# Inverse softmax sums carried as rows through DRAM, and two raw weight pieces fetched first, in a one-core attention and feed-forward kernel

## The chip, the cores and the metric

The kernel runs on one core of a Trainium2 chip. The metric is the device time of one execution in microseconds; the time of a kernel is the median of several runs. The engines are called as the profile calls them: PE (TensorE matmuls), PEld (its weight loads), DVE (VectorE), ACT (ScalarE), POOL (GpSimd) and SP (SyncE, which issues every DMA of this program, in order).

## The reference, cut to what matters

```python
# 8 batches x 8 heads, 576 positions, head size 64, all float32
scores = scale * q @ k.T
cum = np.cumsum(np.log(np.clip(f, 1e-4, 1)), axis=-1)
scores = where(causal, -1e9, scores + cum[..., :, None] - cum[..., None, :])
attn = np.exp(scores - scores.max(-1, keepdims=True))
attn = attn / (attn.sum(-1, keepdims=True) + 1e-9)
x = (attn @ v) -> (4608 tokens, 512)
h = x @ w_in            # 512 -> 2048
out = np.maximum(0.01 * h, h) @ w_out   # 2048 -> 512
```

The division by the row sums is what the change moves. Softmax itself is not normalised when the probabilities are made: the kernel multiplies the finished product `attn @ v` by the inverse sums.

## The kernel before, in words

**Exactness by halves.** A float32 operand is split into a rounded part (`_h`, `ph`, `gh`, `xh`) and a remainder (`_l`, `pl`, `gl`, `xs`), and a product takes two or three matmuls. The weights arrive as 64-bit words. `load_weight(n)` makes the two float32 halves of one piece (there are 16, each of 512 KB, alternately from `w_in` and `w_out`): two DMAs into a buffer `wraw`, one ACT operation (L150) and one ACT cast (L155), and six DVE operations of 1024 columns (L151, L152, L156, L158, L162, L163).

**Opening.** While the first data arrive PE runs dummy matmuls (`warm`, L105). Then come 12 pairs of *early heads* (three batches, the first 256 positions; `early_load`, `early_scores`, `early_values`), with the weight pieces made between them: one piece beside each of the first eight pairs, two beside each of the last four. `early_load` brings `qk` and `ve`; `early_scores` needs `qk` and the decay operand `both`.

**Main part.** 64 tasks follow, one a head; a step of the loop handles the scores of task t and the values of task t-1. For row blocks i = 0 to 4 the step runs `transposes(t-1, i)` and `scores(t, i)`, with pieces of feed-forward work between them (`fill`), then `values(t-1)` on PE, then `split(t+1)`, which makes the halves of the next head's operands and copies some of them by DMA into `fixed_s2a/b` and `fixed_m2a/b`. 24 tasks (of the batches whose first 256 positions were done early) start at block 2; their 12 pairs are called *narrow* here (320 columns), the other 20 pairs *wide* (576 columns). Two heads share an output tile `x` (64 partitions each).

**Inverse sums.** ACT's exponential (L366) leaves the row sums of both heads of a pair in `fixed["sum"]`, positions on the partitions. The products stand the other way round, positions along the columns. Before the change `inverse` takes the reciprocal on DVE (L440, L441, 128x10) and lets POOL repeat each number 64 times into a tile `rw` (L448); `normalise` then transposes `rw` on PE, one 128x128 transpose for each 128 positions, into PSUM tiles `rb` of the tag `tr` (L459), and DVE multiplies `x` by them (L460). The result goes by DMA to `xd` in DRAM (L464), from which the feed-forward part fetches groups of 256 tokens (`xs`, L475).

**Feed-forward.** `ffn` yields small quanta: `h` matmuls (L508, 128x256), an ACT activation, the halves `gh` (DVE, L518) and `gl` (POOL, L520), and `o` matmuls (L541, 128x512). A fixed rule (`fill`) sets how many quanta stand after each block.

**Order.** Within an engine instructions run in the order in which they stand in the program. That order is made by a scheduler with costs of its own, so a change in one place can move instructions elsewhere.

Of the kernel before, what the change touches and what calls it, by code (L numbers as in the profile page):

```python
# [29 lines left out]
RAWS = ("ph", "pl")  # L30
# [6 lines left out]
def forgetting_attention_ffn(ctx, tc, qT, kT, v4, vr, f, w_in, w_out, out):  # L37
# [6 lines left out]
    nc = tc.nc  # L44
    NHEAD, D, S = qT.shape
# [4 lines left out]
    NFULL = S // P  # L50
    REST = S - NFULL * P
    NCH = NFULL + 1
# [59 lines left out]
    ident = ident_r.bitcast(F32)  # L112
# [6 lines left out]
    )  # L119

    xd = dram.tile([DM, NTOK], F32, name="xd")
    dec_k, dec_q = (dram.tile([NHEAD, 2, S], F32, name=n) for n in ("dec_k", "dec_q"))

    fr = one.tile([2 * NHEAD, S], F32, tag="z4", name="fr")
# [6 lines left out]
    wpieces, loaded = [], []  # L131
    wi, wo = w_in.bitcast(I32), w_out.bitcast(I32)
    for p in range(NFC // 2):
        wpieces.append(((wi[p, 0], wi[p, 1]), win_h[p], win_l[p]))
        wpieces.append(((wo[2 * p], wo[2 * p + 1]), wout_h[p], wout_l[p]))

    def load_weight(n):


        loaded.append(n)  # L140
        srcs, wh, wl = wpieces[n]
        wh, wl = (w.rearrange("p c f -> p (c f)") for w in (wh, wl))
        raw = one.tile([P, 2, 4 * P, 2], I32, tag=RAWS[n % 2], name=f"wraw_{n}")
        for k, src in enumerate(srcs):
            nc.sync.dma_start(raw[:, k].rearrange("p w two -> p (w two)"), src)
        raw = raw.rearrange("p m w two -> p (m w) two")
        lo, hi = raw[:, :, 0], raw[:, :, 1]
        t = one.tile([P, 8 * P], I32, tag="vs", name=f"wt_{n}")
        tf = t.bitcast(F32)
        nc.scalar.activation(tf, hi.bitcast(F32), AF.Abs, scale=REBIAS)  # L150
        nc.vector.tensor_scalar(t, t, 3, None, op0=ALU.logical_shift_left)  # L151
        nc.vector.scalar_tensor_tensor(  # L152
            t, hi, -0x80000000, t, op0=ALU.bitwise_and, op1=ALU.bitwise_or
        )
        nc.scalar.copy(wh, tf)  # L155
        nc.vector.tensor_scalar(hi, t, -0x800000, None, op0=ALU.bitwise_and)  # L156
        rest = lo.bitcast(F32)
        nc.vector.scalar_tensor_tensor(  # L158
            rest, lo.bitcast(U32), 2.0**-52, hi.bitcast(F32), op0=ALU.mult, op1=ALU.mult
        )  # L160
        hi = hi.bitcast(F32)
        nc.vector.tensor_tensor(hi, tf, wh.bitcast(F32), op=ALU.subtract)  # L162
        nc.vector.tensor_tensor(wl, hi, rest, op=ALU.add)  # L163

    def weights(n):
        while len(loaded) < min(n, len(wpieces)):
            load_weight(len(loaded))
# [23 lines left out]
    for i in range(NCH):  # L191
        c = slice(i * P, width(i))
# [3 lines left out]
    for name, tag, x, to in (("fck", "s1", fc, dec_k), ("fcq", "m1", start, dec_q)):  # L196
        r = one.tile([P, S], F32R, tag=tag, name=name, bufs=2)
# [5 lines left out]
    pairs = {}  # L203
# [95 lines left out]
    fixed = {}  # L299
# [38 lines left out]
    def scores(t, i):  # L338

        s, c0, c1 = tasks[t]  # L340
        h = state[t]
        m, n = rows(i), width(i)
        if i < NFULL:
            z = h[f"z{i}"] = one.tile([P, n], F32, tag=f"z{i}", name=f"z{i}_{t}")
        else:
            z = h[f"z{i}"] = fixed["z4"]
        z = z[:m, :n]
        if i == c0:
            h["max"] = one.tile([P, NCH + 1], F32, tag="max", name=f"max_{t}", bufs=3)
        parts = [(0, n)] if n <= 512 else [(0, n // 2), (n // 2, n)]  # L350
        for x, (a, b) in enumerate(parts):
            ps = psum.tile([P, 512], F32, tag="sc", name=f"sc_{t}_{i}_{x}")
            cols = slice(i * P, i * P + m)
            for y, w in enumerate("12"):
                nc.tensor.matmul(  # L355
                    ps[:m, :b - a], h["s" + w][:, cols], h["m" + w][:, a:b],
                    start=y == 0, stop=y == 1,
                )
            at = TRI - P - i * P + a
            nc.vector.tensor_tensor_reduce(  # L360
                out=z[:, a:b], in0=ps[:m, :b - a], in1=tri[:m, at:at + b - a], scale=-SCALE,
                scalar=3.0e38 if x == 0 else h["max"][:m, i:i + 1],
                op0=ALU.add, op1=ALU.min, accum_out=h["max"][:m, i + x:i + x + 1],
            )
        last = i + len(parts) - 1
        nc.scalar.activation(  # L366
            z, z, AF.Exp, bias=h["max"][:m, last:last + 1], scale=-1.0,
            accum_out=fixed["sum" + "ab"[s // 2 % 2]][:m, i, s % 2:s % 2 + 1],
        )
# [65 lines left out]

    def inverse(t):

        s, c0, c1 = tasks[t]
        r = one.tile([P, NCH, 2], F32, tag="r", name=f"r_{t}")
        nc.vector.tensor_scalar(r, fixed["sum" + "ab"[s // 2 % 2]], 1.0e-9, None, op0=ALU.add)  # L440
        nc.vector.reciprocal(r, r)  # L441
        wide = pairs[s // 2, c0]["r"] = {}
        for lo, hi in spans(t):
            c = (hi - lo + P - 1) // P
            w = one.tile([P, c, 2, D], F32, tag=f"part{lo == 0:d}", name=f"rw_{t}_{lo}")
            a = r[:, lo // P:lo // P + c]
            a = bass.AP(tensor=a.tensor, offset=a.offset, ap=[*a.ap, [0, D]])
            nc.gpsimd.tensor_copy(w, a)  # L448
            wide[lo] = w.rearrange("p c o d -> p c (o d)")

    def normalise(t):

        s, c0, c1 = tasks[t]
        pair = pairs[s // 2, c0]
        x, r = pair["x"], pair["r"]
        for part, (lo, hi) in enumerate(spans(t)):
            ps = psum.tile([P, 512], F32, tag="tr", name=f"rb_{t}_{part}")
            for c in range(lo, hi, P):
                nc.tensor.transpose(ps[:, c - lo:c - lo + P], r[lo][:, (c - lo) // P], ident)  # L459
            nc.vector.tensor_tensor(x[:, lo:hi], x[:, lo:hi], ps[:, :hi - lo], op=ALU.mult)  # L460
        b, hp = s // HPB, (s % HPB) // 2
        a, n = c0 * P, width(c1 - 1)
        at = place[b, a]
        nc.sync.dma_start(xd[hp * P:(hp + 1) * P, at:at + n - a], x[:, a:n])  # L464

    def spans(t):
        a, n = tasks[t][1] * P, width(tasks[t][2] - 1)
        return [(a, n)] if n - a <= 512 else [(a + P, n), (a, a + P)]
# [137 lines left out]
    for t in range(nt + 1):  # L606
        heads[0] = t < nt
        if t + 1 < nt:
            load(t + 1)
        before = list(range(*tasks[t - 1][1:])) if t else []  # L610
        now = list(range(*tasks[t][1:])) if t < nt else []
        have = ready[0] // T * NQ - used[0]
        left = min((e + 2 - t for e in ends if e + 1 >= t), default=1)
        step = min(have / (left + SLACK), MAXQ) / 8
        fill(step)
        for i in range(5):
            if i in before:
                transposes(t - 1, i)
            if i in now:
                scores(t, i)  # L620
            fill(step)
        if t:
            for part in range(len(spans(t - 1))):
                if part == 0 and tasks[t - 1][0] % 2:
                    inverse(t - 1)
                values(t - 1, part)
                fill(step)
            if tasks[t - 1][0] % 2:
                normalise(t - 1)
# [41 lines left out]
```

## Time and profile before

| | us |
|---|---|
| median of 3 runs | 1243.0 |
| all runs | 1247.97, 1238.74, 1243.0 |
| the profiled execution | 1237.03 |
| span of its instructions | 1235.3 |
| granted TensorE clock | 1.0 throughout |

The profile is one execution. Its page gives the busy time of each engine, 40 time slices, and the chain of work that ended last. Views of the trace give groups of instructions (busy time, mean length of one, idle time before them), an engine's rows in order of time (start, length, name, count, and in brackets the idle time before it and what ended it), what ended each wait, and busy times by stretch. A matmul's record is longer than the time after which the next one starts, since matmuls overlap; the distance between two starts is read from the rows in order of time.

### The profile page before, as it was taken

The numbers are of one execution on the slowest core, as the hardware profiler recorded it, in microseconds if no ns is written. First come the engines' busy times: TensorE is split into PE (matmuls) and PEld (weight loads), VectorE is DVE, ScalarE is ACT, GpSimd is POOL, SyncE is SP. The second block draws the span as 40 slices with busy tenths as digits, with TensorE's granted clock in tenths as the row PEclk, the third lists the DMA queues.
The fourth block names the chain that finished last, engine by engine and source line by source line (L and its number), as shares of the span: only waits on it lengthen the run. The fifth ranks groups of instructions, "written<-read, shape, count | busy, mean of one in ns | idle before, by whom it ended". The sixth has DMA issues, their size and how long they took to land.

```text
span 1235.3 us, 21918 instructions
## 1 busy us (share of the span) xinstructions
PE 1219.8 (99%) x7980; PEld 1077.1 (87%) x7980; DVE 609.6 (49%) x1598; ACT 635.2 (51%) x1511; POOL 444.0 (36%) x395
## 2 busy tenths in 40 slices
PE   9999999999999999999999999999999999999998
PEld 6777788888888989899899999999999998889997
DVE  6888975665554444444434434344343334443211
ACT  6775646667755565555544545454444444651111
POOL 2000254555444344543444443443344334432000
PEclk9999999999999999999999999999999999999999
DMA  6453433343232223322221222221222222211000
GB/s 195 149 168 134 140 100 101 91 119 111 80 113 67 69 84 86 99 69 86 78 86 49 79 69 80 66 77 46 74 73 68 64 61 80 57 53 40 18 18 18
DMA packets 70219, 102.47 MB, mean 83 GB/s; under 512 B 13152, under 2 KB 42384, under 8 KB 70112
## 3 DMA queue, kind: packets, MB, share of 16 engines
q1 hardware_dynamic: 70112, 101.08, 27.3%
q8 instruction: 63, 1.03, 0.4%
q14 instruction: 44, 0.36, 0.1%
HBM read 74.76 MB, written 18.42 MB: 75 GB/s over the span
## 4 chain that ended last, share of the span: by engine, by line
PE 84%; DMA 5%; issue 3%; DVE 3%; ACT 2%; POOL 2%; SPq 1%; POOLq 0%; ACTq 0%; DVEq 0%
PE h L508 29%; PE o L541 29%; PE sc L355 8%; PE av L424 7%; PE tr L382 6%; DMA xs<-xd 2%; PE sce L246 1%; PE rb L459 1%; PE ave L288 1%; DMA xd<-x 1%; DMA kraw<-in_kT 1%; PE sce L249 1%; ACT wt L150 1%; PE warm L105 1%; POOL s L129 1%
## 5 line engine op out<-in xcount | busy, mean ns | idle before, releaser
L508 PE MATMUL h<-xh,win_h 128*128 128x256 f32 x1152 | 331.2, 288 | 0.1
L508 PE MATMUL h<-xh,win_l 128*128 128x256 f32 x1152 | 326.0, 283 | 0.0
L508 PE MATMUL h<-xs,win_h 128*128 128x256 f32 x1024 | 289.2, 282 | 0.0
L520 POOL TENSOR_TENSOR gl<-g,gh 128x512 fp32r<-128x512 f32 x111 | 143.0, 1289 | 307.8 <-DVE gh L518 307.7
L541 PE MATMUL o<-wout_h,gh 128*128 128x512 f32 x576 | 231.0, 402 | 1.5 <-DVE gh L518 1.5
L541 PE MATMUL o<-wout_l,gh 128*128 128x512 f32 x576 | 226.0, 393 | 0.1
L541 PE MATMUL o<-wout_h,gl 128*128 128x512 f32 x576 | 224.8, 392 | 0.7 <-DVE gl L520 0.7
L508 PEld LDWEIGHTS h<-xh,win_h 128*128 128x128 f32 x1152 | 219.4, 191 | 4.4 <-ACT win_h L155 0.5
L508 PEld LDWEIGHTS h<-xh,win_l 128*128 128x128 f32 x1152 | 219.5, 190 | 0.9 <-issue 0.7
L515 ACT ACTIVATE g<-h 128x512 f32<-128x512 f32 x144 | 85.9, 597 | 229.2 <-PE h L508 220.8
L508 PEld LDWEIGHTS h<-xs,win_h 128*128 128x128 f32 x1024 | 195.1, 191 | 3.0
L395 ACT CAST ph<-tr 128x256 fp32r<-128x256 f32 (+3 forms) x272 | 119.5, 445 | 143.2 <-PE tr L382 141.8
L360 DVE CUSTOM_DVE_ANT_0 z<-sc,tri 128x128 f32<-128x128 f32 (+1 forms) x208 | 107.4, 518 | 166.1 <-PE sc L355 166.1
L518 DVE CAST gh<-g 128x512 fp32r<-128x512 f32 x144 | 76.6, 532 | 181.8 <-ACT g L515 179.0
L366 ACT ACTIVATE z<-z,max 128x128 f32<-128x128 f32 (+1 forms) x208 | 122.7, 590 | 79.8 <-DVE max L360 78.7
L397 DVE TENSOR_TENSOR pl<-tr,ph 128x256 fp32r<-128x256 f32 (+3 forms) x272 | 136.7, 508 | 41.4 <-ACT ph L395 41.2
L129 POOL TENSOR_TENSOR s<-qraw,s 64x576 fp32r<-64x576 f32 (+1 forms) x64 | 79.4, 1240 | 182.2 <-ACT s L326 164.5
L541 PEld LDWEIGHTS o<-wout_h,gl 128*128 128x128 f32 x576 | 108.1, 188 | 24.7 <-DVE gl L520 1.2
L355 PE MATMUL sc<-m,s 128*64 128x288 f32 (+1 forms) x336 | 123.2, 372 | 1.8 <-DVE max L360 1.8
L541 PEld LDWEIGHTS o<-wout_h,gh 128*128 128x128 f32 x576 | 108.4, 189 | 18.0 <-DVE gh L518 1.7
L541 PEld LDWEIGHTS o<-wout_l,gh 128*128 128x128 f32 x576 | 108.5, 189 | 16.3 <-issue 0.3
L382 PE MATMUL tr<-ident_r,z 128*128 128x128 f32 x568 | 96.1, 273 | 1.7 <-DVE pl L397 1.1
(112 smaller groups left out, 1807.8 us busy)
## 6 DMA issues: line engine op xcount, KB each, us to landing
kraw<-in_kT SPq DMA_DIRECT2D x128, 144.0 KB
qraw<-in_qT SPq DMA_DIRECT2D x80, 144.0 KB
wraw<-in_w_in SPq DMA_DIRECT2D x16, 512.0 KB
wraw<-in_w_out SPq DMA_DIRECT2D x16, 512.0 KB
fixed_vm<-in_v SPq DMA_DIRECT2D x32, 256.0 KB
xs<-xd SPq DMA_DIRECT2D x16, 512.0 KB
out<-ost SPq DMA_DIRECT2D x28, 256.0 KB
xd<-x SPq DMA_DIRECT2D x20, 288.0 KB
```

The costliest lines, as they stand in the source:

```text
L129: nc.gpsimd.tensor_tensor(out, a, b, op=ALU.subtract)
L355: nc.tensor.matmul(ps[:m, :b - a], h["s" + w][:, cols], h["m" + w][:, a:b], start=y == 0, stop=y == 1,)
L360: nc.vector.tensor_tensor_reduce(out=z[:, a:b], in0=ps[:m, :b - a], in1=tri[:m, at:at + b - a], scale=-SCALE, scalar=3.0e38 if x == 0 else ...
L366: nc.scalar.activation(z, z, AF.Exp, bias=h["max"][:m, last:last + 1], scale=-1.0, accum_out=fixed["sum" + "ab"[s // 2 % 2]][:m, i, s % 2: ...
L382: nc.tensor.transpose(ps[:, x * m:(x + 1) * m], z[:m, j * P:(j + 1) * P], ident[:m, :m])
L395: nc.scalar.copy(o, src)
L397: nc.vector.tensor_tensor(o, src, hi.bitcast(F32), op=ALU.subtract)
L424: nc.tensor.matmul(ps[:, a - lo:hi - lo], fixed["vs"][:, odd, j, :], h[w][:, at:at + hi - a], start=(n == 0), stop=(n == len(steps) - 1),)
L508: nc.tensor.matmul(ph[:, e, :], w[:, c, fs], xx[:, c, :], start=(c == 0 and x == 0), stop=(c == NCC - 1 and x == 2),)
L515: nc.scalar.activation(g, ph, AF.Prelu, alpha=0.01)
L520: eng.tensor_tensor(gl, g, gh.bitcast(F32), op=ALU.subtract)
L541: nc.tensor.matmul(acc[k], gg[:, e, ts], w[:, e, :], start=(fc_ == 2 * p0 and x == 0), stop=(fc_ == 2 * p1 - 1 and x == 2),)
```

## The change

Two parts.

**Inverse sums as rows.** `inverse` still takes the reciprocals on DVE, in a tile ordered by head first. One PE transpose for a pair (`rt`, L455, 10 rows of 128) turns them into rows, ACT copies these from PSUM to SBUF (L459), one DMA writes them to a small DRAM buffer (`rows`, L461), and four DMAs (L464) read them back, each row onto 64 partitions: two into `rb` (the first 512 positions, or 256 of them in a narrow pair), two into `rbr` (the last 64). `normalise` has no PE work any more; DVE multiplies `x` by these SBUF tiles (L475). `inverse` is called after block 1 of the step instead of ahead of `values`.

**Raw words first.** The DMAs of a weight piece are split off as `fetch_weight`, and those of pieces 0 and 1 are issued ahead of the early heads' operands.

```diff
+    rows_d = [dram.tile([2, NCH * P], F32, name=f"rows_{x}") for x in range(4)]
...
+    def fetch_weight(n):
+        raw = raws[n] = one.tile([P, 2, 4 * P, 2], I32, tag=RAWS[n % 2], name=f"wraw_{n}")
+        for k, src in enumerate(wpieces[n][0]):
+            nc.sync.dma_start(raw[:, k].rearrange("p w two -> p (w two)"), src)
...
-        raw = one.tile([P, 2, 4 * P, 2], I32, tag=RAWS[n % 2], name=f"wraw_{n}")
-        for k, src in enumerate(srcs):
-            nc.sync.dma_start(raw[:, k].rearrange("p w two -> p (w two)"), src)
+        if n not in raws:
+            fetch_weight(n)
...
+    for n in range(len(RAWS)):
+        fetch_weight(n)
...
     def inverse(t):
-        r = one.tile([P, NCH, 2], F32, tag="r", name=f"r_{t}")
+        r = one.tile([P, 2, NCH], F32, tag="r", name=f"r_{t}")
...
-            nc.gpsimd.tensor_copy(w, a)
+        ps = psum.tile([P, 512], F32, tag="tr", name=f"rt_{t}")
+        nc.tensor.transpose(ps[:2 * NCH, :P], r.rearrange("p o c -> p (o c)"), ident)
...
+        nc.scalar.copy(flat, ps[:2 * NCH, :P])
+        to = rows_d[s // 2 % 4]
+        nc.sync.dma_start(to.rearrange("o (c q) -> (o c) q", q=P), flat)
+        for y, lo, hi in ((main[:, c0 * P:], c0 * P, NFULL * P), (rest[:, :REST], NFULL * P, S)):
+            for o in range(2):
+                nc.sync.dma_start(
+                    y[o * D:(o + 1) * D], to[o:o + 1, lo:hi].broadcast_to([D, hi - lo])
+                )
...
     def normalise(t):
-            for c in range(lo, hi, P):
-                nc.tensor.transpose(ps[:, c - lo:c - lo + P], r[lo][:, (c - lo) // P], ident)
-            nc.vector.tensor_tensor(x[:, lo:hi], x[:, lo:hi], ps[:, :hi - lo], op=ALU.mult)
+            nc.vector.tensor_tensor(x[:, lo:hi], x[:, lo:hi], y, op=ALU.mult)
...
+            if i == 1 and t and tasks[t - 1][0] % 2:
+                inverse(t - 1)
             fill(step)
         if t:
             for part in range(len(spans(t - 1))):
-                if part == 0 and tasks[t - 1][0] % 2:
-                    inverse(t - 1)
                 values(t - 1, part)
```

How it moves instructions is shown at three places. SP first, from the start of the program; `fr` is the forget input, `wraw` the raw weight words, `qk` and `ve` the early heads' operands, `dec_k` and `dec_q` decay rows that SP writes once POOL has made them. Before:

```order
L126 DMA fr<-in_f 64x576 x2
L228 DMA qk_0_171<-in_qT 128x256
L228 DMA qk_0_171<-in_kT 128x256
L232 DMA ve_0_174<-in_v 128x2x128
L228 DMA qk_1_176<-in_qT 128x256
L228 DMA qk_1_176<-in_kT 128x256
L232 DMA ve_1_179<-in_v 128x2x128
L145 DMA wraw_223<-in_w_in 128x1024 x2
L200 DMA dec_k<-fck 64x576 x2
```

And now:

```order
L127 DMA fr<-in_f 64x576 x2
L143 DMA wraw_135<-in_w_in 128x1024 x2
L143 DMA wraw_138<-in_w_out 128x1024 x2
L238 DMA qk_0_181<-in_qT 128x256
L238 DMA qk_0_181<-in_kT 128x256
L210 DMA dec_k<-fck 64x576 x2
L210 DMA dec_q<-fcq 64x576 x2
L242 DMA ve_0_184<-in_v 128x2x128
L238 DMA qk_1_186<-in_qT 128x256
L238 DMA qk_1_186<-in_kT 128x256
```

Both weight pieces (1 MB) moved ahead of the first pair's operands, and the second pair's fell behind the two waits for POOL. Next DVE, where its opening meets the first early scores: `start` belongs to the decay rows, `ze_0` and `maxe_0` are the scores of the first pair taken from PSUM, `wt` and `wraw` the weight piece. Before:

```order
L193 TENSOR_SCALAR start<-fc 128x64
L259 ISA ze_0_0_189,maxe_0_181<-sce_0_0_183,tri 128x128
L259 ISA maxe_0_181 128x1
L259 ISA ze_0_2_192,maxe_0_181<-sce_0_2_184,tri 128x128
L259 ISA maxe_0_181 128x1
L259 ISA ze_0_1_206,maxe_0_181<-sce_0_1_200,tri 128x256
L259 ISA maxe_0_181 128x1
L259 ISA ze_0_3_209,maxe_0_181<-sce_0_3_201,tri 128x256
L259 ISA maxe_0_181 128x1
L151 TENSOR_SCALAR wt_226<-wt_226 128x1024
```

And now:

```order
L203 TENSOR_SCALAR start<-fc 128x64
L158 TENSOR_SCALAR wt_233<-wt_233 128x1024
L159 SCALAR_TENSOR_TENSOR wt_233<-wraw_135,wt_233 128x1024
L163 TENSOR_SCALAR wraw_135<-wt_233 128x1024
L165 SCALAR_TENSOR_TENSOR wraw_135<-wraw_135 128x1024
L269 ISA ze_0_0_199,maxe_0_191<-sce_0_0_193,tri 128x128
L269 ISA maxe_0_191 128x1
L269 ISA ze_0_2_202,maxe_0_191<-sce_0_2_194,tri 128x128
L269 ISA maxe_0_191 128x1
L169 TENSOR_TENSOR wraw_135<-wt_233,win_h_93 128x1024
```

Four of the first piece's six operations now stand ahead of the first scores, and the fifth among them. PE moved with it: before, 20 dummy matmuls stood ahead of the first `sce` matmul; now 40 do (their number in all, 68, is unchanged). Last the first narrow pair's inverse sums, on SP; `fixed_s2a` and `fixed_m2a` are operands of the next step's scores, `qraw` and `kraw` later heads' inputs, `x` the pair's product. Before:

```order
L213 DMA qraw_2076<-in_qT 64x320 x2
L213 DMA kraw_2079<-in_kT 64x576 x2
L329 DMA fixed_s2a<-dec_q 2x320
L328 DMA fixed_s2a<-s_4_2191 64x320
L330 DMA fixed_m2a<-dec_k 2x576
```

And now:

```order
L223 DMA qraw_2085<-in_qT 64x320 x2
L223 DMA kraw_2088<-in_kT 64x576 x2
L461 DMA rows_126<-rbr_1965 10x128
L464 DMA rb_1964<-rows_126 64x256 x2
L464 DMA rbr_1965<-rows_126 64x64 x2
L339 DMA fixed_s2a<-dec_q 2x320
L338 DMA fixed_s2a<-s_4_2200 64x320
L340 DMA fixed_m2a<-dec_k 2x576
```

The write and the four reads stand ahead of the next head's operand copies. The same holds for the wide pairs. On PE the one transpose `rt` stands six `o` matmuls ahead of the step's first transposes in this pair, and between the scores of block 1 and the transposes of block 2 in a wide pair.

More of the change, by code (lines that the diff above doesn't have):

```diff
@@ L135, in forgetting_attention_ffn @@
         wpieces.append(((wo[2 * p], wo[2 * p + 1]), wout_h[p], wout_l[p]))
+    raws = {}
+    def fetch_weight(n):
+        raw = raws[n] = one.tile([P, 2, 4 * P, 2], I32, tag=RAWS[n % 2], name=f"wraw_{n}")
+        for k, src in enumerate(wpieces[n][0]):
+            nc.sync.dma_start(raw[:, k].rearrange("p w two -> p (w two)"), src)
     def load_weight(n):
         loaded.append(n)
-        srcs, wh, wl = wpieces[n]
+        _, wh, wl = wpieces[n]
         wh, wl = (w.rearrange("p c f -> p (c f)") for w in (wh, wl))
-        raw = one.tile([P, 2, 4 * P, 2], I32, tag=RAWS[n % 2], name=f"wraw_{n}")
-        for k, src in enumerate(srcs):
-            nc.sync.dma_start(raw[:, k].rearrange("p w two -> p (w two)"), src)
-        raw = raw.rearrange("p m w two -> p (m w) two")
+        if n not in raws:
+            fetch_weight(n)
+        raw = raws[n].rearrange("p m w two -> p (m w) two")
         lo, hi = raw[:, :, 0], raw[:, :, 1]
@@ L438, in inverse @@
         s, c0, c1 = tasks[t]
-        r = one.tile([P, NCH, 2], F32, tag="r", name=f"r_{t}")
-        nc.vector.tensor_scalar(r, fixed["sum" + "ab"[s // 2 % 2]], 1.0e-9, None, op0=ALU.add)
+        r = one.tile([P, 2, NCH], F32, tag="r", name=f"r_{t}")
+        sums = fixed["sum" + "ab"[s // 2 % 2]].rearrange("p c o -> p o c")
+        nc.vector.tensor_scalar(r, sums, 1.0e-9, None, op0=ALU.add)
         nc.vector.reciprocal(r, r)
[L442 to L447, printed above, removed]
-            nc.gpsimd.tensor_copy(w, a)
-            wide[lo] = w.rearrange("p c o d -> p c (o d)")
+        ps = psum.tile([P, 512], F32, tag="tr", name=f"rt_{t}")
+        nc.tensor.transpose(ps[:2 * NCH, :P], r.rearrange("p o c -> p (o c)"), ident)
+        main = one.tile([P, NFULL * P], F32, tag="part0", name=f"rb_{t}")
+        rest = one.tile([P, 2 * P], F32, tag="part1", name=f"rbr_{t}")
+        flat = rest[:2 * NCH, P:]
+        nc.scalar.copy(flat, ps[:2 * NCH, :P])
[6 more added lines that the diff above has]
+                )
+        pairs[s // 2, c0]["r"] = main, rest
     def normalise(t):
@@ L454, in normalise @@
         pair = pairs[s // 2, c0]
-        x, r = pair["x"], pair["r"]
-        for part, (lo, hi) in enumerate(spans(t)):
-            ps = psum.tile([P, 512], F32, tag="tr", name=f"rb_{t}_{part}")
-            for c in range(lo, hi, P):
-                nc.tensor.transpose(ps[:, c - lo:c - lo + P], r[lo][:, (c - lo) // P], ident)
-            nc.vector.tensor_tensor(x[:, lo:hi], x[:, lo:hi], ps[:, :hi - lo], op=ALU.mult)
+        x, (main, rest) = pair["x"], pair["r"]
+        for y, lo, hi in ((main[:, c0 * P:], c0 * P, NFULL * P), (rest[:, :REST], NFULL * P, S)):
+            nc.vector.tensor_tensor(x[:, lo:hi], x[:, lo:hi], y, op=ALU.mult)
         b, hp = s // HPB, (s % HPB) // 2
```

## The prediction

> **What bounds the kernel now.** I read the busy times first, then the chain of work that ended last, by engine and by line.
>
> ```profile
> PE 1219.8 (99%) x7980; PEld 1077.1 (87%) x7980; DVE 609.6 (49%) x1598; ACT 635.2 (51%) x1511; POOL 444.0 (36%) x395
> ...
> PE 84%; DMA 5%; issue 3%; DVE 3%; ACT 2%; POOL 2%; SPq 1%; POOLq 0%; ACTq 0%; DVEq 0%
> PE h L508 29%; PE o L541 29%; PE sc L355 8%; PE av L424 7%; PE tr L382 6%; DMA xs<-xd 2%; PE sce L246 1%; PE rb L459 1%; PE ave L288 1%; DMA xd<-x 1%; DMA kraw<-in_kT 1%; PE sce L249 1%; ACT wt L150 1%; PE warm L105 1%; POOL s L129 1%
> ```
>
> PE is busy for 99% of the span and makes up 84% of the chain; DVE, ACT and POOL are busy for half or less. So an instruction taken from PE is worth the time for which it holds PE, one taken from POOL or put on ACT is worth nothing, and a new wait counts only as far as PE runs out of other work. The chain gives the transposes `rb` 1% of the span, some 12 us.
>
> The stretches at the two ends of the early part differ. Columns: stretch, length, busy PE, PEld, DVE, ACT and POOL with counts, granted clock, DMA share, GB/s.
>
> ```profile
> 0.00:10.00 10.00, 8.54 (x29) 6.61 (x30) 4.33 (x11) 3.15 (x5) 2.35 (x11) 1.00 0.64 183
> 10.00:20.00 10.00, 8.38 (x38) 4.97 (x37) 7.18 (x23) 6.91 (x16) 3.46 (x4) 1.00 0.64 191
> 140.00:160.00 20.00, 17.64 (x111) 15.02 (x110) 18.80 (x22) 10.12 (x19) 10.05 (x13) 1.00 0.39 125
> ```
>
> From 10 to 20 us PE stands still for 1.62 us, and between 140 and 160, where the last weight pieces are made, for 2.36 with DVE busy for 18.80 of 20. That is all that an earlier start of the weight work could win: 4.0 us.
>
> **What is removed.** First the group of the transposes (busy us, mean ns | idle before), then what PE waited for ahead of them, then PE's rows around one wide pair's five.
>
> ```profile
> L459 PE MATMUL rb<-ident_r,rw 128*128 128x128 f32 x136 | 21.8, 277 | 0.4 <-DVE x L432 0.4
> ```
>
> ```profile
>   DVE x L432: 1.6, 6
>   issue: 0.4, 2
> ```
>
> ```profile
> 716.76 0.71 PE L459 MATMUL rb<-ident_r,rw 128*128 128x128 f32 x5
> 717.22 0.48 PE L541 MATMUL o<-wout_h,gh 128*128 128x512 f32 x1
> 717.54 0.40 PE L541 MATMUL o<-wout_l,gh 128*128 128x512 f32 x1
> 717.77 0.40 PE L541 MATMUL o<-wout_h,gl 128*128 128x512 f32 x1
> ```
>
> 136 transposes go: five for each of 20 wide pairs, three for each of 12 narrow ones. A record is 277 ns long, but they overlap: the five start at 716.76, the next matmul at 717.22, 0.46 us later. That matmul then needs 0.32 (717.22 to 717.54) instead of the 0.23 of its neighbour (717.54 to 717.77), so the group costs 0.46 + 0.09 = 0.55 us, 0.109 for one. 136 × 0.109 = **14.8 us**. This agrees with the chain's 1%. The waits ahead of them come to 2.0 us in these lines; some of that would be filled elsewhere, and I take **1 us** (0 to 2). POOL's repeating copies go as well, beside PE, for nothing: POOL was at 36%.
>
> The Trainium skill, page "TensorE: Matmul & The Clock Gate", section "Part 4: PE-mode transpose", gives about 275 ns for one 128x128 transpose in a kernel's context. The trace agrees with that as a record's length (277) and not as the time that PE is held (109); by the page's figure the net 104 transposes would be worth an estimated 28.6 us.
>
> **What is added on PE and ACT.** 32 transposes `rt` with 10 rows. Nothing of that shape is in the trace; the nearest rows are a lone 128x128 transpose and what follows it, and for the copy to SBUF an ACT copy of 64x128.
>
> ```profile
> 721.57 0.27 PE L382 MATMUL tr<-ident_r,z 128*128 128x128 f32 x1
> 721.60 0.31 PE L355 MATMUL sc<-m,s 128*128 128x128 f32 x1
> ```
>
> ```profile
> L431 ACT COPY y<-av 64x128 f32<-64x128 f32 x40 | 10.4, 261 | 30.9 <-PE av L424 18.9 <-DVE x L432 11.6
> ```
>
> The lone transpose lets its neighbour start after 0.03 us; a whole record is 0.277. So 32 cost 1.0 to 8.9 us; I take the 0.109 of the group, the nearest kind, **3.5 us**. ACT gets 32 × 0.26 = 8.3 us at 51% busy: nothing. A `rt` tile also takes a slot in PSUM that the next `tr` would have had, with the scores and feed-forward matmuls of the step between to cover it; I price that at nothing, bounded by the waits below.
>
> **The way through DRAM.** Each pair now writes its rows and reads them back, two transfers in a row. The chain has both kinds; columns are start, length, what.
>
> ```profile
> 341.09 4.09 DMA xd<-x
> ...
> 1035.10 2.40 DMA xd<-x
> ```
>
> ```profile
> 136.14 3.27 DMA kraw<-in_kT
> ...
> 252.06 5.34 DMA kraw<-in_kT
> ```
>
> A write to DRAM lands 2.4 to 4.1 us after its issue, a read 3.3 to 5.3: together **5.7 to 9.4 us**, plus issues on SP of about 0.55 each (a row below, two in 1.10). The Trainium skill, page "DMA: Bandwidth & Descriptors", section "Anatomy of one DMA — SWDGE (gpsimd) path", puts the fixed cost at about 2 us, mostly the receipt of the write, heaviest in HBM: "This can cause a surprisingly long delay especially when the write target is HBM." That speaks against the change; two hops by it are an estimated 4 us, and the rows of this case are longer still.
>
> In a wide pair there is room. ACT, SP and DVE in the step before 716.76:
>
> ```profile
> 703.84 0.37 ACT L395 CAST ph<-tr 128x256 fp32r<-128x256 f32 x1 [0.85 <-PE tr L382]
> ```
>
> ```profile
> 702.46 1.15 SPq L557 DMA_DIRECT2D out<-ost  x2
> 710.93 0.23 SPq L329 DMA_DIRECT2D fixed_s2a<-dec_q  x1
> ```
>
> ```profile
> 714.39 0.63 DVE L432 TENSOR_TENSOR x<-av,y 64x448 f32<-64x448 f32 x1 [2.43 <-ACT y L431]
> ```
>
> `rt` stands just ahead of the transposes whose cast starts at 703.84, so the rows are in SBUF by about 704.5. SP stands free from 703.6 to 710.93. The write lands by 706.9 to 708.6, four reads are issued by 709.1 to 710.8, and land by 710.2 (the first) to 713.9 at the latest (the first two) or 716 (all). The product needs them after 714.39 + 0.63 = 715.0. Nothing waits, or at worst 1 us on the last 64 columns, with `h` and `o` matmuls queued on PE.
>
> A narrow pair is tight. The first of them, on DVE, ACT, PE and SP:
>
> ```profile
> 178.44 0.76 DVE L440 TENSOR_SCALAR r<-fixed_suma 128x10 f32<-128x10 f32 x1 [2.00 <-ACT fixed_z L366]
> 179.23 0.22 DVE L441 RECIPROCAL r<-r 128x10 f32<-128x10 f32 x1
> ...
> 187.80 0.49 DVE L432 TENSOR_TENSOR x<-av,y 64x320 f32<-64x320 f32 x1 [1.44 <-ACT y L431]
> 188.70 0.49 DVE L460 TENSOR_TENSOR x<-x,rb 128x320 f32<-128x320 f32 x1 [0.41 <-PE rb L459]
> ```
>
> ```profile
> 179.24 0.60 ACT L515 ACTIVATE g<-h 128x512 f32<-128x512 f32 x1
> ```
>
> ```profile
> 181.01 0.38 PE L382 MATMUL tr<-ident_r,z 128*128 128x128 f32 x2
> ```
>
> ```profile
> 179.19 1.10 SPq L213 DMA_DIRECT2D kraw<-in_kT  x2
> 185.32 0.23 SPq L329 DMA_DIRECT2D fixed_s2a<-dec_q  x1
> ```
>
> The reciprocals end at 179.45. `rt` stands six `o` matmuls of 0.23 ahead of 181.01, that is at 179.6: 0.2 us later, so PE just does not wait; if the reciprocals slip, those six wait behind `rt`. ACT's copy comes after `g` (179.84), by 180.1. The write, issued then, lands by 182.5 to 184.2; the first two reads, issued 0.55 and 1.1 after, land by 186.3 to 190.1. DVE needs them at 188.3: a wait of 0 to 1.8 us, up to 2.9 for the last read. Queued on SP behind the reads stand the next step's operand copies: they started at 185.32 and now start after 184.7 to 186.4, up to 1.1 late, with a head's `sc` waiting for them. Queued on DVE behind the waiting multiply is the cast `gh`, for which `o` waits. But PE has that step's `h` and `o` quanta in front, and SP has mostly time to spare:
>
> ```profile
> SPq L329 <- PE sc L355: 399.5, 59, 13.2
> ```
>
> SP waited for scores ahead of these copies for 399.5 us in 59 cases, 6.8 each, more than five issues of 0.55. Waits for the rows cost PE 0 to 8 us in all; as the middle of the windows is a wait of under 1 us for 12 pairs, mostly covered, I take **+1**.
>
> **The opening.** PE's and DVE's rows before:
>
> ```profile
> 1.46 7.03 PE L105 MATMUL warm<-still 128*128 128x512 f32 x20 [1.46 <-DVE still L96]
> 8.41 0.49 PE L246 MATMUL sce<-qk 64*128 64x128 f32 x4
> 8.84 2.11 PE L105 MATMUL warm<-still 128*128 128x512 f32 x8
> ```
>
> ```profile
> 12.02 0.28 DVE L259 CUSTOM_DVE_ANT_0 ze<-sce,tri 128x128 f32<-128x128 f32 x1
> ...
> 16.02 0.69 DVE L151 TENSOR_SCALAR wt<-wt 128x1024 int32<-128x1024 int32 x1 [1.63 <-ACT wt L150]
> ...
> 17.12 1.23 DVE L152 SCALAR_TENSOR_TENSOR wt<-wraw,wt 128x1024 int32<-128x1024 int32 x1
> ```
>
> Twenty more dummies, at (2.11 − 0.40)/7 = 0.24 each, put the first scores 4.9 us later, at 13.3. The words and the forget input, at 183 GB/s about 8 us for the first 1.5 MB, are there by then. Four weight operations (two like 0.69, two like 1.23, 3.8 us) now run on DVE ahead of the first scores, which leave PSUM at about 16 instead of 12.02. The same 3.8 us are gone from later, and DVE's 1.63 idle ahead of 16.02 is filled. So the opening loses about 4 us for scores and gains the weight work; the early part is bound by DVE, and I expect the weights to end sooner. Bounds: −4 (both stretches' idle time won) to +4 (scores late and nothing won back); I take **−2**, half the gain, since DVE's work is the longer line.
>
> **Sum.** −14.8 − 1 + 3.5 + 1 − 2 = **−13.3 us**. The profiled execution took 1237.0, so it would be 1223.7. The median of the three runs shown is 1243.0, 6 us above the profiled one; from it, 1229.7. About 1% is what a measurement of this kernel can tell from no change (the three runs span 0.7%), that is 12.4 us: the forecast lies on that line.
>
> **Rivals.**
> - *Rows late, PE partly idle.* For: the narrow pair's windows. At 0.7 us for 12 pairs, 8.4 in place of +1, the sum is −5.9: 1237. Against: PE's queue of feed-forward work. Chance 0.13.
> - *Rows late enough to be slower than before.* One mechanism: DVE's multiply in the narrow pairs waits for the last read, `gh` behind it is late, and PE has no matmul left. The rest of the sum is −14.3, so from 1.2 us of idle PE for each of 12 pairs on the kernel is slower than before; 2.2 make it slower by 1%; the worst, 2.9, gives 35 − 14.3 = +21, 1264. Chance 0.06.
> - *The opening costs its 4 us.* −14.8 − 1 + 3.5 + 1 + 4 = −7.3: 1236. For: scores come 4 us later. Against: DVE at 18.80 of 20 at the far end. Chance 0.08.
> - *A transpose holds PE for its whole record.* 104 net at 0.277 are 28.8: −28.8 − 1 + 1 − 2 = −30.8, 1212. For: the record. Against: the starts. Chance 0.07. The Trainium skill's section on the transpose, cited above, is the page with this rule.
> - *Nothing comes of it.* If PE's time is set elsewhere, the freed PE time turns into waiting: 1243. Against: 99% busy. Chance 0.04.
>
> **How the numbers follow.** The forecast has 0.62, with a range of its own of 1220 (`rt` at 0.03, the opening at −4, no wait, and 2 of waits gone gives −20.8, 1222, and some run noise) to 1236 (`rt` at its record gives +5.4, 1235). Two thirds of it (0.41) is below 1230.6, as its likeliest deviations, a cheap `rt` and no waits, point down; with the whole-record case **0.48 faster**. Same: 0.21 + 0.13 + 0.08 + 0.04 = **0.46**. Slower **0.06**. The range 1218 to 1242 leaves out the slower case, the case of no effect and most of the whole-record case, 0.17.
>
> **What would show it.** `rb` gone from PE, `rt` with starts 0.03 to 0.28 before the next matmul and little idle time ahead of it; DVE's multiply in wide pairs not waiting for a DMA, in narrow pairs up to 1.8 us; SP's operand copies no more than 1 us later; the first `sce` at about 13 us, the last weight operation sooner. I am wrong if PE's idle time in the narrow steps grows by more than 1 us each, if `rt` waits for the reciprocals, or if PE idles more before 160 than now.

## The result, and the profile after

| | kernel before | changed kernel |
|---|---|---|
| median (us) | 1240.9 of 4 | 1227.7 of 4 |
| all runs | 1236.1 to 1248.0 | 1227.2 to 1229.3 |
| profiled execution | 1237.0 | 1227.2 |
| span | 1235.3 | 1225.4 |
| mean granted clock in it | 1.000 | 0.994 |

The ratio is 0.9886, with a 95% interval of 0.985 to 0.9922: faster by 1.1%, 13.2 us between the medians against 13.3 forecast. But between the two profiled executions, on which the sum was made, it is 9.9 us. So the total came out right while terms in it did not, and the experiments had to say which. One execution of before in a later session, at 2119.9 us with a granted clock of 0.775, is left out of all comparisons.

The page of the changed kernel, at the places shown of before:

```profile
PE 1208.4 (99%) x7876; PEld 1069.0 (87%) x7876; DVE 638.2 (52%) x1610; ACT 642.3 (52%) x1543; POOL 432.0 (35%) x343
...
PE 89%; DMA 3%; DVE 3%; ACT 1%; issue 1%; POOL 1%; SPq 1%; ACTq 0%; POOLq 0%; DVEq 0%
```

PE has 104 instructions fewer and is still busy for 99%. DVE is busy for 28.6 us more, though it was given nothing new: that was not forecast.

The line of the `tr` transposes (count, shortest/median/longest ns, first and last start) cuts the span into the opening and the main part. Before, then after:

```profile
L382 PE MATMUL tr<-ident_r,z x568: 270/272/328, 171.1 to 1119.6; 128*128 128x128 f32 x190
```

```profile
L392 PE MATMUL tr<-ident_r,z x568: 269/272/447, 167.4 to 1110.0; 128*128 128x128 f32 x190
```

The opening is 3.7 us shorter. The main part, from the first to the last start, went from 948.5 to 942.6: 5.9 us, where the prediction's terms for it (−14.8 − 1 + 3.5 + 1) give 11.3. About 5.4 us are missing there. PE's waits and three stretches after (us, times, longest; then busy PE, PEld, DVE, ACT, POOL, granted clock, DMA share, GB/s) show where:

```profile
PE tr L392 <- DVE pl L407: 4.0, 2, 3.0
PE sce L256 <- DVE maxe L269: 2.5, 2, 2.4
PE tr L392 <- DVE x L442: 1.8, 1, 1.8
```

```profile
250.00:260.00 10.00, 8.14 (x53) 7.04 (x52) 5.98 (x17) 5.25 (x14) 6.68 (x5) 0.93 0.40 111
260.00:270.00 10.00, 10.00 (x62) 8.69 (x62) 5.20 (x17) 6.98 (x17) 3.99 (x4) 0.90 0.28 77
360.00:370.00 10.00, 8.66 (x44) 7.83 (x45) 4.78 (x14) 5.34 (x12) 4.72 (x4) 0.66 0.37 116
```

Two stalls of PE, 1.8 us at 256 and 3.0 at 358, are followed by a lower granted clock; in the profiled execution of before it was 1.00 in these stretches. In steps of 2 us behind the longer stall:

```profile
358.00:360.00 2.00, 0.32 (x2) 0.00 (x0) 2.00 (x4) 1.45 (x4) 1.76 (x1) 1.00 0.00 0
360.00:362.00 2.00, 0.66 (x3) 0.69 (x4) 2.00 (x5) 0.30 (x1) 1.64 (x2) 0.75 0.51 183
362.00:364.00 2.00, 2.00 (x10) 1.23 (x10) 0.82 (x4) 1.36 (x4) 0.22 (x1) 0.50 0.41 134
364.00:366.00 2.00, 2.00 (x10) 1.97 (x10) 1.55 (x7) 1.55 (x4) 0.00 (x0) 0.50 0.28 100
366.00:368.00 2.00, 2.00 (x11) 1.99 (x10) 0.35 (x2) 1.61 (x4) 1.58 (x2) 0.55 0.30 69
368.00:370.00 2.00, 2.00 (x17) 1.96 (x16) 0.06 (x1) 0.53 (x1) 1.28 (x1) 1.00 0.34 91
```

After the stall the clock is at half for some 7 us: PE, fully busy, starts 10 or 11 matmuls in 2 us and then 17. That is (1 − 0.66) × 10 = 3.4 us of full clock lost there, and 0.7 + 1.0 = 1.7 behind the first stall. Stalls and lost clock come to 1.8 + 3.0 + 3.4 + 1.7 = 9.9 us; before, PE had waited 0.5, 1.0 and 1.1 us at these places. The growth is 7.3 us, enough for the 5.4 that are missing. The opening is not free of it either: behind 36 us the changed kernel's execution ran at half clock for some 3 us, which cost it another 1.7.

### The profile page after: what moved, and what is told of

It is laid out like the page before. It is cut to its first block, busy times and chain, and to the rows that moved or that the text cites. A ratio compares the mean times of both kernels' runs of the same rounds, so it can differ in the third digit from the quotient of the medians.

```text
span 1225.4 us, 21897 instructions
## 1 busy us (share of the span) xinstructions
PE 1208.4 (99%) x7876; PEld 1069.0 (87%) x7876; DVE 638.2 (52%) x1610; ACT 642.3 (52%) x1543; POOL 432.0 (35%) x343
## 4 chain that ended last, share of the span: by engine, by line
PE 89%; DMA 3%; DVE 3%; ACT 1%; issue 1%; POOL 1%; SPq 1%; ACTq 0%; POOLq 0%; DVEq 0%
PE h L523 32%; PE o L556 31%; PE sc L365 8%; PE av L434 7%; PE tr L392 7%; DMA xs<-xd 1%; PE sce L256 1%; DMA kraw<-in_kT 1%; DMA xd<-x 1%; PE ave L298 1%; PE sce L259 1%; DVE wraw L165 1%; PE tre L289 1%; DVE wt L159 0%; DMA wraw<-in_w_in 0%
```

## The experiments

**One part at a time.** The rows with the old opening, and the raw words with the old division:

```diff
 rows_only (from the changed kernel)
-    for n in range(len(RAWS)):
-        fetch_weight(n)
 words_only (from the kernel before)
+    for n in range(len(RAWS)):
+        fetch_weight(n)
```

> The inverse sums as rows through DRAM, with the opening of the kernel before. Theory A (the net price of the PE work removed is 0.109 us for a transpose rb and 0.03 for an rt, and the opening won 3.7 us by itself): about 1231 us, that is 3 to 4 us over the changed kernel, PE's first tr at 171 us again, and the two stalls of PE at the ends of batches (around 259 and 362 us) with the half clock behind them still there. Theory B (the removed transposes held PE for a whole record of 0.277 and the way through DRAM gives most of it back in waits spread over the pairs): the same total, but PE idle time of 0.3 to 1 us in most of the 32 steps with a product.

> The raw words of two pieces first, with the inverse sums as in the kernel before. Theory A: the opening is worth 3.7 us by itself, so about 1237 us against 1241 of the kernel before, the first tr near 167.4 instead of 171.1. Rival: the early gain belongs to the other part or is lost again at the ends of batches: within 1 us of the kernel before.

`rows_only`: 1232.8 (ratio 0.995, 0.9916 to 0.9985). `words_only`: 1232.6 (0.9924, 0.9894 to 0.9953). Both against 1240.1, the median of 25 executions of before. So by the medians each half is worth about 7.4 us (by the ratios 6.2 and 9.4): the rows less than the 11.3 forecast for them, the words more than 2 and more than the 3.7 that one profile showed. The two stalls come with the rows: `rows_only` has them at 2.1 and 2.3 us, `words_only` at 0.4 and 1.1 as before. Theory A missed for the words (1237) by 4 us. Why, the opening of `rows_only`'s profiled execution (1242 us, a long one) says. Four stretches:

```profile
10.00:20.00 10.00, 7.53 (x30) 4.46 (x30) 7.27 (x23) 6.79 (x16) 3.58 (x4) 0.91 0.60 166
20.00:30.00 10.00, 10.00 (x32) 6.05 (x31) 5.13 (x13) 4.92 (x14) 0.00 (x0) 0.50 0.29 92
30.00:40.00 10.00, 10.00 (x30) 6.14 (x29) 4.82 (x12) 5.43 (x17) 0.85 (x1) 0.57 0.44 145
40.00:50.00 10.00, 9.93 (x48) 6.26 (x47) 8.38 (x18) 7.45 (x21) 1.30 (x1) 1.00 0.55 177
```

The old opening leaves PE idle for 2.5 of the 10 us from 10 on, and in this execution 20 us at half clock followed; its first `tr` came at 182.9 instead of 171.1. The profiled execution of before had been spared. Over 25 executions of before, the time follows the mean clock: 1235.1 to 1236.4 where it was 1.000, 1238.1 to 1240.1 at 0.997, 1247.6 to 1248.8 at 0.989.

**Is it the clock?** The kernel before, with its gaps in the opening filled:

```diff
 more_warm (from the kernel before)
-                warm(WARM[1])
+                warm(WARM[1] + (4 if b * HPB // 2 + g < 2 else 0))
```

> The kernel before with 16 more dummy matmuls in the first two early pairs, which fill PE's idle time between 10 and 17 us, and nothing else. Theory A (the spread of the kernel before, 1235 to 1249 us, comes from a granted clock of 0.5 that follows those gaps in some executions, and a good part of what the raw words won is that they take these gaps away): most executions at 1235 to 1237, clock 1.0, a median some 4 us under that of the kernel before. Rival (the opening is won by the earlier weights alone): the median of the kernel before, 1240, or the 16 dummies later at 0.23 each, 1244.

1236.4 (ratio 0.9953, 0.9926 to 0.998), all ten executions at 0.998 to 1.000 and between 1234.3 and 1239.4, beside 1235.2 to 1249.6 of before. 16 dummy matmuls that compute nothing win 6.4 us at the median and shrink the spread to about a third. Theory A holds: the old opening lost several us in most executions to the clock.

**A price for a transpose.**

```diff
 double_rb (from the kernel before)
-                nc.tensor.transpose(ps[:, c - lo:c - lo + P], ...)
+                for _ in range(2):
+                    nc.tensor.transpose(ps[:, c - lo:c - lo + P], ...)
```

> The kernel before with each of the 136 transposes rb made twice, into the same place: a price for them alone. Theory A (0.109 us each, from the distance of starts): +14.8 us, about 1256. Theory B (a whole record of 0.277 each): +37.7 us, about 1279.

1253.5: +13.3 us (ratio 1.0093, 1.005 to 1.0136), 0.098 for each of 136 (0.05 to 0.12 by the interval). Its rows on PE around one wide pair agree:

```profile
724.43 1.25 PE L460 MATMUL rb<-ident_r,rw 128*128 128x128 f32 x10
725.44 0.47 PE L542 MATMUL o<-wout_h,gh 128*128 128x512 f32 x1
```

Ten take 1.01 us from start to start. The whole-record price (+37.7) lies far outside the interval.

**Is the way through DRAM just hidden?** `inverse` back at its old place, ahead of the values:

```diff
 late_rows (from the changed kernel)
-            if i == 1 and t and tasks[t - 1][0] % 2:
-                inverse(t - 1)
...
             for part in range(len(spans(t - 1))):
+                if part == 0 and tasks[t - 1][0] % 2:
+                    inverse(t - 1)
```

> The changed kernel with the inverse sums made and sent only ahead of the values, where the kernel before had them. Theory A (the rows' way takes 5.7 to 9.4 us and is hidden only because it starts after block 1): DVE's multiply waits some 2 to 6 us in each of 32 pairs, half of it or less reaches PE: 1235 to 1290 us, in the middle 1250. Rival (the way through DRAM is hidden anyway, since PE has feed-forward work queued and DVE nothing urgent behind the multiply): 1228 us, as the changed kernel.

1227.2 (ratio 0.9886, 0.9817 to 0.9955), as the changed kernel: the rival was right. DVE's waits in it:

```profile
DVE x L475 <- DMA rb<-rows: 46.3, 26, 5.2
DVE x L475 <- DMA rbr<-rows: 6.1, 11, 1.2
```

Here DVE does wait for the rows, up to 5.2 us and 52.4 in all, and little of it reaches PE: after the opening PE stands still for 7.6 us against 6.5 in the changed kernel. It does so at other places. The longest of these stalls is 1.8 us at 939, with half clock behind it; at the two places of the changed kernel's stalls PE waits no more than 0.7 us. In the changed kernel no wait for the rows is listed. The early place of `inverse` is not what makes the change work, and my fear of late rows was for nothing.

**The two stalls.** A repeat of the changed kernel, and a try to move the cast in which DVE waits:

> The changed kernel unchanged, as the measure for the three beside it, and a second look at its two stalls (PE idle 1.8 us at 256 and 3.0 at 358, each followed by a granted clock of 0.5). Theory A (they belong to the order of the program): the same two in the same places, 1227 us. Rival (they are accidents of one execution): they move or go.

1228.1, with stalls of 2.3 us at 257 and 2.6 at 360: they belong to the program.

```diff
 delay5 (from the changed kernel)
-DELAY = 3
+DELAY = 5
```

> The changed kernel, with the cast xh of a fetched group of tokens two quanta later in the program (a constant of 3 is 5). Theory A (PE's two stalls come from DVE, which waits in that cast 2.4 and 4.0 us for the transfer of xs, with the scores' reductions behind it): DVE waits less there, the stalls and the half clock behind them go, 1219 to 1224. Rival (PE has no other work in that time, so the wait only moves to the matmuls h): 1226 to 1230.

Inconclusive: with the constant at 5 every engine's instructions stand in the same order as with 3, so this was the changed kernel once more (1228.1).

Then DVE's rows at the first stall. Each row's end in brackets is the idle time and what ended it. Of before, around the last narrow pair of the first batch, and then of the changed kernel:

```profile
246.88 0.49 DVE L432 TENSOR_TENSOR x<-av,y 64x320 f32<-64x320 f32 x1 [1.44 <-ACT y L431]
247.48 0.49 DVE L460 TENSOR_TENSOR x<-x,rb 128x320 f32<-128x320 f32 x1
...
256.59 0.69 DVE L480 CAST xh<-xs 128x1024 fp32r<-128x1024 f32 x1 [1.53 <-DMA xs<-xd]
```

```profile
242.76 0.49 DVE L442 TENSOR_TENSOR x<-av,y 64x320 f32<-64x320 f32 x1 [1.44 <-ACT y L441]
243.28 0.84 DVE L475 TENSOR_TENSOR x<-x,rb 128x256 f32<-128x256 f32 x1
244.05 0.90 DVE L475 TENSOR_TENSOR x<-x,rbr 128x64 f32<-128x64 f32 x1
...
253.31 0.83 DVE L495 CAST xh<-xs 128x1024 fp32r<-128x1024 f32 x1 [2.39 <-DMA xs<-xd]
```

From the sum `x` to the end of the multiply it takes 244.95 − 242.76 = 2.2 us instead of 1.1. The product goes to `xd` and comes back as `xs`, so from the sum to the cast it takes 10.55 us instead of 9.71. That is 0.84 of the 1.3 us by which this stall of PE grew; the three transposes that PE no longer does there, about 0.3, are another part. DVE waits 2.39 instead of 1.53 in the cast, and behind the cast stand the reductions and sums for which PE's next transposes wait. The multiply is longer since POOL is in the middle of an operation when it begins. POOL's rows there, and DVE's last multiply of the program, for which POOL is idle:

```profile
242.40 1.44 POOL L130 TENSOR_TENSOR fixed_m2a<-kraw,m 64x576 fp32r<-64x576 f32 x1
243.92 0.94 POOL L130 TENSOR_TENSOR fixed_vs<-fixed_vm,fixed_vs 128x320 fp32r<-128x320 f32 x1
```

```profile
1114.62 0.43 DVE L475 TENSOR_TENSOR x<-x,rb 128x256 f32<-128x256 f32 x1
1114.96 0.22 DVE L475 TENSOR_TENSOR x<-x,rbr 128x64 f32<-128x64 f32 x1
```

0.43 and 0.22 alone, 0.84 and 0.90 beside POOL. To test whether this makes the stalls, the last pair of each batch is divided in the old way, out of PSUM:

```diff
 ends_by_pe (from the changed kernel)
+    def inverse_pe(t):
...
+            nc.gpsimd.tensor_copy(w, a)
...
     def normalise(t):
+        if s % HPB == HPB - 1:
...
+                    nc.tensor.transpose(ps[:, c - lo:c - lo + P], r[lo][:, (c - lo) // P], ident)
+                nc.vector.tensor_tensor(x[:, lo:hi], x[:, lo:hi], ps[:, :hi - lo], op=ALU.mult)
...
+                if part == 0 and tasks[t - 1][0] % HPB == HPB - 1:
+                    inverse_pe(t - 1)
                 values(t - 1, part)
```

> The changed kernel, but the last pair of each batch (8 of 32) is divided as in the kernel before: repeated by POOL, transposed on PE (34 transposes rb, +3.5 us net at 0.109), multiplied by DVE out of PSUM. Theory A (the multiply out of SBUF, 0.84 + 0.90 instead of 0.49 us beside POOL, makes xd, xs and xh of a batch's end late, and the stall at 256 us comes from it): that stall is back at about 0.5 us and the clock stays at 1.0 behind it, 1225 to 1229 in all. Rival (the stall comes from PE having less to do ahead of it, whatever divides): it stays, and the time is 1231.

1224.4 (ratio 0.9863, 0.981 to 0.9917). The stalls are 0.42 and 0.65 us, and the clock stays up behind them:

```profile
246.92 0.49 DVE L494 TENSOR_TENSOR x<-x,rb 128x320 f32<-128x320 f32 x1
...
255.92 0.70 DVE L517 CAST xh<-xs 128x1024 fp32r<-128x1024 f32 x1 [1.44 <-DMA xs<-xd]
```

```profile
260.00:270.00 10.00, 9.72 (x61) 8.01 (x62) 6.29 (x20) 8.34 (x22) 4.87 (x5) 1.00 0.29 77
...
360.00:370.00 10.00, 9.36 (x63) 8.11 (x63) 6.99 (x18) 6.55 (x15) 5.46 (x5) 1.00 0.46 145
```

```profile
L392 PE MATMUL tr<-ident_r,z x568: 270/272/328, 171.1 to 1108.3; 128*128 128x128 f32 x190
```

The main part takes 937.2 us, 5.4 less than in the changed kernel, although PE does 34 transposes `rb` more and 8 `rt` less. The gain does not show in this execution's total (1226.6), since its opening lost some 7 us to half clock, from 18 to 24 us and from 38 to 50; the two of the four at a mean clock of 0.999 and 1.000 took 1222.0 and 1223.5. This kernel is the fastest so far, so it was timed again:

> The same kernel as ends_by_pe, timed in more rounds, since it was the fastest so far. Theory A (dividing the last pairs of the batches in the old way takes the two stalls away, worth 3 to 4 us over the changed kernel): 1223 to 1226, PE idle no more than 0.7 us at either place. Rival (its first four executions were lucky ones): 1227 to 1229, as the changed kernel.

1225.0 (0.9853, 0.9813 to 0.9893), PE idle 0.8 us at the first place and none at the second. But it changes the multiply, the way of the rows, the place of `inverse` and PE's work at once. PE's work alone:

```diff
 ends_cover (from the changed kernel)
-        nc.tensor.transpose(ps[:2 * NCH, :P], ..., ident)
+        for _ in range(4 * (c1 - c0) + 1 if s % HPB == HPB - 1 else 1):
+            nc.tensor.transpose(ps[:2 * NCH, :P], ..., ident)
```

> The changed kernel, where the transpose rt of a batch's last pair (8 of 32) is made 13 or 21 times instead of once, so that PE gets some 0.35 or 0.6 us more to do in those steps, about what the transposes rb took; DVE, the rows and the multiply stay as they are. Theory A (the stalls come from the lengthened multiply and the chain xd, xs, xh behind it): both stalls stay, at 1.5 to 2.5 us, with the half clock behind them, and the time is 1228 to 1232. Rival (PE's missing cover is the cause, and the transposes rb were only that): the stalls shrink to about 0.5 us as with the last pairs divided in the old way, 1224.

1242.0. The extra work was three times what I meant it to be. Thirteen `rt` in one narrow pair:

```profile
236.71 1.58 PE L456 MATMUL rt<-ident_r,r 128*10 128x128 f32 x13 [0.47 <-DVE r L453]
238.05 0.48 PE L557 MATMUL o<-wout_h,gh 128*128 128x512 f32 x1
```

They take 1.34 us, 0.103 each: the 0.03 to the next start after a lone one, on which I had sized this, is not its price, since the matmul behind is late then. The 136 extra ones cost 14.3 us over the changed kernel, 0.105 each (13 us by the ratios to before). With 1.3 us more for PE the first stall shrank to 0.7 with the multiply as long as ever (0.86 and 0.89); the second stayed at 2.2, with the clock at 0.71 behind it. So the cover closes the first stall, at its full price; with a quarter of it, the old way of dividing closes both.

The lengthened multiply explains the first stall by its rows, but only together with the place of the cast in DVE's order. In `late_rows` even more time passes there from the sum to the cast, 12.6 us, and PE waits only 0.4 and 0.7 us; that cast stands behind the reductions.

It does not explain the second. DVE's rows there, of before and of the changed kernel (`z` is the reduction of a block's scores):

```profile
339.62 0.82 DVE L460 TENSOR_TENSOR x<-x,rb 128x448 f32<-128x448 f32 x2 [0.19 <-PE rb L459]
...
348.75 0.69 DVE L480 CAST xh<-xs 128x1024 fp32r<-128x1024 f32 x1 [3.15 <-DMA xs<-xd]
349.35 0.68 DVE L360 CUSTOM_DVE_ANT_0 z<-sc,tri 128x512 f32<-128x512 f32 x1
...
360.87 0.69 DVE L480 CAST xh<-xs 128x1024 fp32r<-128x1024 f32 x1 [1.92 <-DMA xs<-xd]
```

```profile
336.11 0.89 DVE L475 TENSOR_TENSOR x<-x,rb 128x512 f32<-128x512 f32 x1
...
342.56 0.69 DVE L370 CUSTOM_DVE_ANT_0 z<-sc,tri 128x512 f32<-128x512 f32 x1 [1.26 <-PE sc L365]
...
345.58 0.69 DVE L495 CAST xh<-xs 128x1024 fp32r<-128x1024 f32 x1 [1.72 <-DMA xs<-xd]
...
357.46 0.69 DVE L495 CAST xh<-xs 128x1024 fp32r<-128x1024 f32 x1 [3.98 <-DMA xs<-xd]
```

From the start of the first sum `x` (338.19 and 334.83) to the end of the multiply (340.44 and 337.00) it takes 2.2 us in both. From one cast to the next it takes 12.1 us before, 11.9 in the changed kernel and 11.7 in `ends_by_pe`: the second fetch of `xs` stands on SP behind inputs whose buffers POOL has to free first (in the changed kernel POOL is done with the two at 350.15 and 351.75, and SP issues their DMAs at 350.18 and 351.78). What differs is when DVE comes to the second cast: 10.2 us after the first in before and in `ends_by_pe`, 7.9 in the changed kernel, where the reduction of 512 columns stands ahead of the first cast and not behind it. The rest is DVE's wait: 1.92 us, 1.55 in `ends_by_pe` and 3.98 in the changed kernel. PE's stall follows it. So the second stall goes with the order of DVE's instructions, which `ends_by_pe` changes back. No run changed the multiply alone or that order alone; for the second stall the cause is read from rows and not tested.

**Both findings together.**

```diff
 ends_old_open (from ends_by_pe: the old opening, 16 dummies more)
-    for n in range(len(RAWS)):
-        fetch_weight(n)
...
-                warm(WARM[1])
+                warm(WARM[1] + (4 if b * HPB // 2 + g < 2 else 0))
 best_8_2 (from ends_by_pe: the new opening, 32 dummies more)
-                warm(WARM[1])
+                warm(WARM[1] + (8 if b * HPB // 2 + g < 2 else 0))
```

> The rows for 24 of 32 pairs, the last pairs of the batches divided in the old way, and the opening of the kernel before with 16 more dummies in place of the raw words first. Theory A (the opening's part is for the larger half the clock, which the dummies save too, and for 2 to 3 us the earlier weights): 1225 to 1228, clock 0.999 to 1.0. Rival (the raw words bring the whole of it): 1231 to 1233.

> The raw words first, the rows for 24 of 32 pairs, the last pairs of the batches divided in the old way, and 32 more dummies in the first two early pairs. Theory A (the half clock behind PE's gaps in the opening goes, at no cost, since DVE bounds that part): 1221 to 1224, clock 0.998 to 1.0. Rival (the dummies stand in front of the scores that DVE waits for, or miss the gap at 15 us): 1225 to 1230.

1226.1 (0.9871, 0.9818 to 0.9924) and 1226.6 (0.9868, 0.9825 to 0.9912), mean clocks 0.998 to 1.000 in all eight. With the clock kept up, the raw words first (with 32 dummies) and the old opening with 16 are worth the same within what these runs tell. `best_8_2` missed its 1221 to 1224, although its clock stayed up: the gap at 15 us was still 1.9 us, and `ends_by_pe` without the dummies was no slower.

## Why the prediction was right, and by which steps it was not

- **What is removed: right.** 0.109 us for a transpose `rb` (its own rows, 0.55 / 5, give 0.110); the doubled ones cost 0.098 (0.101 in its rows). At these prices the term is 13.3 to 15.0 us. The 277 ns of a record are no price.
- **What is added on PE: right.** 0.109 for `rt`; a run of 13 shows 0.103, and a lone one 0.11 (in the changed kernel the next `o` starts 0.03 us after it, and the one after that 0.31 later instead of 0.23).
- **The way through DRAM: right that it does not hurt, with the danger put too high.** No multiply waits for a row, and where it does (`late_rows`) the time is the same. In the narrow pair where I had counted a wait of 0 to 1.8 us it was none. The rivals on late rows are out.
- **The waits: the term that was mis-sized, and for another cause.** I took +1 (0 to 8) for rows that land late. From the main part, −14.8 − 1 + 3.5 + w = −5.9 gives w = +6.4; the two stalls at the ends of batches and the half clock behind them grew by 7.3. The prediction counted DVE's multiply at no change and overlooked that it now reads two operands from SBUF beside POOL, which is the first stall. For the second it did not follow DVE's order up to the fetch of `xs`: where that fetch sets the pace, time saved ahead of it is waited away. And it priced a wait at its own length, not with the clock that it takes along.
- **The opening: the other mis-sized term.** −2 (−4 to +4) forecast. The profiled executions give −3.7, the medians −7.5 (`words_only`), since that profile of before was one at full clock. The new opening is not safe either: in the changed kernel's execution 1.7 us went to half clock behind 36 us, in that of `ends_by_pe` some 7. First scores at 13.3 us were forecast, and PE's row has them at 12.88:

```profile
12.88 0.49 PE L256 MATMUL sce<-qk 64*128 64x128 f32 x4
```

- **The frame.** The sum was made against the profiled execution, 1237.0, and carried to the median, 6 us above it, as though the difference were noise. It was half clock in the opening, which the change mends in part. In the profiled frame the forecast was too good by 13.3 − 9.9 = 3.4 us; this and the opening's gain at the median cancelled. That is luck: 1230 against 1227.7 is right for reasons that are half the ones given.
- **A slip in the range.** The terms named for its lower end (−14.8 − 2 + 1.0 + 0 − 4) give −19.8 and not −20.8, so 1223 and not 1222.

## What to carry to other kernels

Before a sum is made on one profiled execution, look at the granted clock of several: a spread of 1% that follows the clock is itself something to win, here with 16 dummy matmuls in two early pairs. When an operand moves from PSUM to SBUF, look at what POOL does at that moment, and follow the result to the next transfer. Compare each engine's order before and after, also where the change does not reach. And an edit that saves everywhere may be worth undoing at the few places where its result is waited for: the old way for 8 of 32 pairs made the changed kernel faster by another 3 us.

## What the runs showed of the hardware

- **Half clock after short gaps.** PE idle for 1.8 us (at 256) and for 3.0 (at 358) was followed by a granted clock of 0.5 for several us, 7 of them after the longer one. In the changed kernel's opening it also came behind 36 us, where the last idle time was only 0.66 us. Idle times of 1.1 us at 364 in before and of 2.4 at 15 us in the changed kernel were not followed by it in those executions, nor was one of 1.5 us near 150 in either. The same opening was followed by 20 us of it in one execution and by none in another. The Trainium skill, page "TensorE: Matmul & The Clock Gate", section "Part 1: The HAM clock gate (the "warmup" mystery)", has the clock fall to half after an idle window of about 3.4 us, in windows that run free of the program. The chance in it agrees with these runs; as a bound 3.4 us does not, since a gap of 1.8 behind dense work was enough.
- **DVE beside POOL.** DVE's multiply with both operands in SBUF took 0.43 us (128x256) and 0.22 (128x64) with POOL idle, and 0.84 and 0.90 beside POOL's operations. What counts in this trace is whether a POOL operation is under way when the multiply begins. All three 128x256 multiplies for which that was so took 0.72 to 0.95 us and ended 0.28 us after POOL's operation; eight others, where POOL's operation began just after them, took 0.43. The 14 of 128x512 that began during one ended 0.55 us after it, and the longest took 2.58 us; the six others took 0.69. The group of the wide pairs averages twice the 0.62 that 128x448 took out of PSUM:

```profile
L475 DVE TENSOR_TENSOR x<-x,rb 128x512 f32<-128x512 f32 x20 | 24.6, 1232 | 0.7
```

  The Trainium skill, page "GPSIMD Engine Reference", section "1. Specifications", says that POOL shares its SBUF interfaces with DVE and contends with DVE instructions that have two SBUF inputs. These rows agree. The groups of the multiply come to 49.8 us after and 23.8 before, 26.0 of DVE's 28.6 more.
